# Smaller products in a tiled TensorE: a long convolution's first and last step, and the block maxima of sliding-window attention, placed on other tiles of the array

## The chip, the cores and the metric

The kernel runs as one program on one core of one Trainium2 chip. The time is device microseconds (us) of one execution. The kernel before was timed in three runs: 959.37, 967.51 and 975.18 us, median 967.51.

## The reference

Two independent results are computed and put side by side in the output, 2048 rows of 2 x 576 columns, all in float32:

```python
# left half: attention, H = 32 heads of Dh = 18, S = 2048, window W = 256
q, k, v = split_heads(x @ wqkv)
scores = einsum("bhqd,bhkd->bhqk", q, k) * Dh ** -0.5      # kept where 0 <= q - k < 256
a = merge_heads(einsum("bhqk,bhkd->bhqd", softmax(scores), v)) @ wo
# right half: a state-space convolution, L = 2048, D = 576 channels, N = 128 states
dt = exp(log_dt)
K[d, l] = sum_n real(C[d, n] * exp(dt * (A_re + 1j * A_im) * l)[d, n] * dt * B[d, n])
y = irfft(rfft(pad(u)) * rfft(pad(K)))[:L] + u * Dskip       # transforms of length 4096
concatenate([a, y], -1)
```

## The kernel before

**Taps and projection.** The taps K of the convolution (2048 of them for each of 576 channels) are made from factors: `tables` has phases and exponentials made by matmuls (L414), VectorE, ScalarE and GpSimd, and `taps` (L522) multiplies the factors on TensorE in tiles of 32 columns. Beside it `proj` makes q, k and v with `mm14` (L180), and stores them to a DRAM table `qd` in half-precision pieces. The attention's operands are later loaded from `qd` in units: a unit is four heads and one half of the queries (1024), 16 units in all, each with a Q tile [128, 2, 1024] and a K tile [128, 2, 1280] (`load_unit`, L715 and L716). A head's 54 rows lie on partitions 0 to 53 or 64 to 117, so that two heads share a tile's column.

**The transform.** The convolution is a Fourier transform of u and of K in two steps (32 x 64), a product, and the two inverse steps.
- `s1` (L555 to L567) is the first step. A block is 4 of the 64 values of l, for 144 channels: a tile `src` of 128 partitions (four groups of channels s, with 32 values each) by 576 columns. `w1` is [128, 2, 128]: for each of the two parts, cosine and sine, a block-diagonal matrix with the same 32x32 block for every group. A block takes four matmuls (two parts, two column chunks of 288), each into a PSUM bank of its own, four evacuations of 288 columns, three in four on ScalarE and one in four on VectorE (`evac`, L142), and one store for each part into DRAM: `gx` for u, `gk` for K. `s1_u` (L569) loads each block of u and runs 16 of them, `s1_k` (L578) runs 16 over the taps. The banks come from the pool `pps`, three banks, as long as the projection's pool lives, later from `ring`.
- `conv` (L584 to L681): 16 steps load 2 of the 32 values of f from `gx` and `gk` (`load`, L592 and L596, one step ahead), do the second step (`s2`, L606), multiply on VectorE and GpSimd (L637 to L644), do the first inverse step (`inverse`, L614), and store to a DRAM table `h`. Then 16 last steps (`qd` is the loop variable here): `loadh` (L658) loads four pieces of `h` three steps ahead; four matmuls (L675) with `i2`, a block-diagonal [128, 64], fill two banks of the ring, one for each half of 576 channels; ScalarE evacuates one and VectorE the other, and four stores write 32 rows of 576 columns each into the output.

**Attention.** For each unit, `gmax` (L722 to L754) makes a bound for the softmax: for each of 32 blocks of 32 queries, the scores against the 288 keys that the block can see, and their row maximum over the masked part. A block has four matmuls (L734), one for each head j, on row half j % 2 of the array (64 rows) and column tile j (32 columns), all into one ring bank. Blocks go in pairs, then VectorE reduces each bank in one custom instruction (L741) into a column of `m`. At a unit's end `m` is scaled and transposed to `mt`, and four stores put each head's 1024 values into row 54 or 118 of the unit's Q tile: the scores matmul (L775) then subtracts the bound by itself. `scores` (L775, exponential on ScalarE at L777, mask on GpSimd at L786), `values` (L798) and the normalization follow in items: 16 units x 2 halves x 3 banks are 96 items. The output's product with wo is spread over the last items (`wo_first`, `wo_part`), and its rest, `wo_rest` (L1008, L1042), runs for the third and the fourth chunk of 512 rows at the very end; its operands `oh` and `ol` are loaded at L996.

**What sets the order.** Up to the attention a scheduler orders the instructions that are handed to it by `merge`, which interleaves generators by shares: `merge((proj, 50), (tables, 308), (s1u, 16))`, a share for each step that the generator yields. From `attention_start` on the order is written out by hand: an item takes two steps of scores, about 2.7 steps (pairs) of `gmax`, one of values, some of `conv`, and for the first nine items one block of `s1_k`. Three blocks' worth of `s1_k` (2 + 2 + 1) stand ahead of the items, beside the maxima of unit 0, and two more ahead of that. The ring has three PSUM banks and serves the maxima, the late `s1_k`, all of `conv` and the wo products.

**DMAs.** Nearly all DMAs are issued by SyncE (SP), one behind the other in program order; an issue that waits holds up all behind it. `after(1, ...)` puts a store off until the next item's beginning (`begin`), so that it doesn't stand in the queue before its data is made. The recorded line of a store is then L134. In the queue, stores of the last step show as `out_dram<-t`, the loads of h as `tx<-h` and `ho<-h`, the maxima's as `Q<-mt`, the first step's as `gx<-g` and `gk<-g`, those of the wo product as `out_dram<-ya`, and `den<-osb` is the normalization's.

## Time and profile before

| | before |
|---|---|
| runs, us | 959.37, 967.51, 975.18; median 967.51 |
| the profiled execution, its own time | 969.41 us |
| its span (first to last instruction) | 967.7 us |
| granted TensorE clock, mean | 0.968 |
| busy: PE (TensorE matmuls) | 845.6 us, 87% |
| busy: DVE (VectorE) | 636.2 us, 66% |
| busy: ACT (ScalarE), POOL (GpSimd) | 565.1 and 565.8 us, 58% each |
| bytes moved, mean rate | 145.45 MB, 150 GB/s |

The profile is one execution as the hardware recorded it. PEld is TensorE's weight load, which overlaps with the matmuls. A view by windows gives the busy time of each engine in stretches of the span with its count of instructions, in the order PE, PEld, DVE, ACT, POOL, then the granted clock, the share of the 16 DMA engines and GB/s. The chain of waits starts at the last instruction of a stretch and goes back at each step to what released it, or to the instruction before it on its engine; by line, it says what share of the stretch each line holds on that chain. "PE r L734" is a matmul of line 734 whose output is named r; "SPq" is SP issuing a DMA; "DMA" is a transfer under way; "issue" is time in which an engine waited for nothing recorded. A timeline row has the start, the duration, the engine, the line, output and inputs, tile shapes and the number of instructions or passes, and behind <- what was waited for. Stages of the span, by where the lines appear: to about 90 us loads and set-up; 90 to 398 tables, projection and `s1_u`; 398 to 430 `s1_k` and the maxima of unit 0; 430 to 485 the first nine items with the rest of `s1_k`; 485 to 850 the middle of the convolution beside the attention; 850 to 968 the last steps and the end.

### The profile page before, as it was taken

To read this page: it belongs to the slowest core of one execution; us is meant where nothing else is said; L and a number is where in the kernel's file an instruction comes from. 1 tells how busy PE (TensorE), PEld (TensorE's weight loads), DVE (VectorE), ACT (ScalarE), POOL (GpSimd) and SP (SyncE) were. 2 spreads that over 40 slices of the span, in tenths; PEclk is the share of its full clock that TensorE was granted. 3 is DMA by queue.
4 is the path that set the end of the run, shared out by engine and by line. 5 is a ranking of instruction groups with operands and counts; after the bars stand their busy time and mean duration, and the time that the engine had idled before them with its cause. 6 is when DMAs were issued, how large, how long until landed. Compare 5 with 4: busy or idle time off the path is not lost.

```text
span 967.7 us, 28844 instructions
## 1 busy us (share of the span) xinstructions
PE 845.6 (87%) x11364; PEld 434.8 (45%) x11364; DVE 636.2 (66%) x1745; ACT 565.1 (58%) x917; POOL 565.8 (58%) x679
## 2 busy tenths in 40 slices
PE   4876789888999899889988988889988999999887
PEld 1344445464566556644423333333333444444345
DVE  5988558467664684556577777887777575666434
ACT  2663766556667676335646556566665555565670
POOL 2178758385685695602357776586876666553360
PEclk9987899899999999999999999999999899999899
DMA  9845345334443443553485676865668475477763
GB/s 326 256 98 147 90 118 134 94 81 125 104 123 92 101 117 84 167 177 131 151 174 146 174 175 164 183 174 135 159 149 197 109 185 152 124 186 200 189 188 132
DMA packets 137184, 145.45 MB, mean 150 GB/s; under 512 B 36552, under 2 KB 105336, under 8 KB 136920
## 3 DMA queue, kind: packets, MB, share of 16 engines
q1 hardware_dynamic: 131000, 131.45, 52.3%
q0 software_dynamic: 4592, 10.32, 4.0%
q8 instruction: 89, 1.46, 0.7%
q10 hardware_dynamic: 1456, 1.84, 0.6%
q14 instruction: 47, 0.39, 0.1%
HBM read 81.29 MB, written 61.01 MB: 147 GB/s over the span
## 4 chain that ended last, share of the span: by engine, by line
PE 50%; DVE 13%; issue 10%; DMA 8%; POOL 7%; ACT 7%; SPq 3%; DVEq 0%; ACTq 0%; POOLq 0%
PE pp L180 8%; PE po L798 6%; PE r L734 6%; PE r L606 6%; PE r L1008 5%; PE kp L522 4%; PE ST L775 4%; PE pp L565 3%; PE r L614 3%; DVE jk L741 2%; PE r L565 2%; PE x L414 2%; DMA raw<-in_x_dram 2%; DMA K<-in_wqkv_dram 2%; PE r L675 1%
## 5 line engine op out<-in xcount | busy, mean ns | idle before, releaser
L741 DVE CUSTOM_DVE_ANT_0 jk<-r,bias 128x288 f32<-128x288 f32 (+7 forms) x512 | 198.8, 432 | 98.0 <-PE r L734 97.3
L786 POOL TENSOR_SCALAR_AFFINE_SELECT P<-P 128x512 f32<-128x512 f32 x240 | 156.7, 681 | 164.2 <-ACT P L777 160.8
L777 ACT ACTIVATE P<-ST,esc 128x1024 f32<-128x1024 f32 (+1 forms) x192 | 201.8, 1059 | 73.1 <-PE ST L775 72.5
L484 POOL TENSOR_TENSOR m<-A,tr 128x1024 f32<-128x1024 f32 x72 | 142.2, 1999 | 73.7 <-PE kp L522 73.6
L734 PE MATMUL r<-K,Q 54*32 54x288 f16 (+8 forms) x2048 | 127.0, 285 | 18.6 <-DVE t L637 4.4
L798 PE MATMUL po<-P,V 128*32 128x256 f32 (+2 forms) x1408 | 100.4, 396 | 12.6 <-ACT osb L806 6.0
L734 PEld LDWEIGHTS <-Q 54*32 54x32 f16 x2048 | 46.3, 90 | 112.5 <-issue 87.6
L643 POOL TENSOR_TENSOR Y<-t,t 64x288 f32<-64x288 f32 x64 | 55.7, 871 | 66.1 <-DVE t L638 64.1
L522 PE MATMUL kp<-Q,m 128*32 128x64 f32 x4608 | 80.4, 222 | 12.8 <-DVE Q L505 3.5
L522 PEld LDWEIGHTS kp<-Q,m 128*32 128x32 f32 x4608 | 69.4, 110 | 37.3 <-issue 23.6
L775 PE MATMUL ST<-Q,K 64*128 64x384 f16 (+2 forms) x704 | 73.8, 281 | 3.4 <-ACT oh L858 1.7
L798 PEld LDWEIGHTS po<-P,V 128*32 128x32 f32 x1408 | 35.7, 110 | 47.1 <-issue 23.8
L565 PE MATMUL pp<-ut,w 128*128 128x288 f32 x128 | 41.1, 452 | 17.1 <-ACT g L145 12.4
L644 POOL TENSOR_TENSOR Y<-t,t 64x288 f32<-64x288 f32 x64 | 52.6, 822 | 3.8
L425 DVE TENSOR_TENSOR k<-x,k 128x512 f32<-128x512 f32 (+1 forms) x54 | 33.9, 642 | 30.0 <-ACT k L424 29.5
L426 DVE TENSOR_SCALAR ab<-k 128x512 int32<-128x512 int32 (+1 forms) x54 | 50.8, 951 | 1.7 <-POOL wr L343 1.3
L606 PE MATMUL r<-tk,w 128*64 128x288 f32 x256 | 42.2, 436 | 7.1 <-DVE m L741 7.1
L462 POOL TENSOR_TENSOR tr<-tr,mab 128x768 f32<-128x768 f32 x18 | 34.6, 1920 | 23.6 <-ACT tr L431 23.5
L614 PE MATMUL r<-Y,i 128*128 128x288 f32 x128 | 42.9, 446 | 5.4 <-DVE m L741 2.3
L606 PE MATMUL r<-tx,w 128*64 128x288 f32 x256 | 40.8, 429 | 7.3 <-DVE m L741 3.8
L431 ACT ACTIVATE mg<-x 128x512 f32<-128x512 f32 x72 | 39.7, 599 | 6.8 <-PE x L414 6.4
L364 DVE SCALAR_TENSOR_TENSOR qst<-pp,qst 128x512 f16<-128x512 f32 x30 | 20.6, 686 | 33.3 <-ACT qst L363 29.6
(190 smaller groups left out, 1664.7 us busy)
## 6 DMA issues: line engine op xcount, KB each, us to landing
qd<-qst SPq DMA_DIRECT2D x72, 128.0 KB
gx<-g SPq DMA_DIRECT2D x32, 288.0 KB
gk<-g SPq DMA_DIRECT2D x32, 288.0 KB
tx<-gx SPq DMA_DIRECT2D x32, 288.0 KB
tk<-gk SPq DMA_DIRECT2D x32, 288.0 KB
h<-ho SPq DMA_DIRECT2D x16, 576.0 KB
Q<-qd SPq DMA_DIRECT2D x32, 216.0 KB
raw<-in_x_dram SPq DMA_DIRECT2D x16, 320.0 KB
```

The lines of the kernel that those rows point to most:

```text
L180: self.nc.tensor.matmul(ps, u, v, start=(i == 0), stop=(i == len(ops) - 1))
L484: self.nc.gpsimd.tensor_tensor(m, A[:, ch, a0:a0 + 8].unsqueeze(3).to_broadcast(sh), tr[:, ch, part, 0:8].unsqueeze(2).to_broadcast(sh), o ...
L522: nc.tensor.matmul(kp[32 * st:32 * st + 32, c % 2 * JJ2 + j, :], m[:, ch, a0:a0 + 32], Q[:, ch, term % 2, :], start=(term == 0), stop=(ter ...
L565: nc.tensor.matmul(ps, self.w1[:, part, :], src[:, o:o + k], start=True, stop=True)
L606: nc.tensor.matmul(ps[64 * par:64 * par + 64], w2[:, par, 64 * part:64 * part + 64], t[:, par, 2 * hs:2 * hs + 2, :], start=True, stop=True)
L614: nc.tensor.matmul(pair[par], i1[:, par, :], Y[par], start=True, stop=True)
L734: nc.tensor.matmul(ps[32 * j:32 * j + 32, :n], d["Q"][r, b, 32 * t:32 * t + 32], d["K"][r, b, k0:k0 + n], start=True, stop=True, skip_grou ...
L741: nc.vector.tensor_tensor_reduce(out=jk[:, :n], in0=ps[:, :n], in1=self.bias[:, 288 - n:], scale=1.0, scalar=-3e38, op0=OP.add, op1=OP.max ...
L775: nc.tensor.matmul(ps[:, u, o:o + n], d["K"][h, jp, k0:k0 + 128], d["Q"][h, jp, q0:q0 + n], start=True, stop=True, skip_group_check=True)
L777: nc.scalar.activation(pt[:, 2 * jp:2 * jp + 2, lo:hi], ps[:, :, lo:hi], AF.Exp, scale=self.esc)
L786: nc.gpsimd.affine_select(v, v, pattern=[[0, 4], [sg, 128]], compare_op=OP.is_ge, fill=0.0, base=-1 if far else 0, channel_multiplier=-sg)
L798: nc.tensor.matmul(self.po[32 * j:32 * j + 32, t0 * 128:t1 * 128], V[:, kb * 76 + 19 * j:kb * 76 + 19 * j + 32], pt[:, j, o:o + (t1 - t0) ...
```

## The change

**First step.** `w1` shrinks to the 32x32 block for each part, repeated for the four row groups ([128, 2, 32]). A block of `s1` is done in two halves of two channel groups each. A half takes two banks, and each bank gets four matmuls of 32 rows by 32 columns with 288 columns moving: group s0 + s on row tile s0 + s, and on the four column tiles the two column chunks lg by the two parts. Eight matmuls stand side by side. Then come two evacuations of 288 columns, and two stores, one for each chunk, of 64 partitions x 2 x 288. A half is a step of its own, so the shares of `s1_u` and `s1_k` double.

**Last step.** `i2` shrinks to [128, 32], the 64x32 block for each row half. The four matmuls of 128x64 become eight of 64x32: row half p, column tile 2k + (p ^ hf), so that in the second bank (hf = 1) the two values of p come out the other way round. The output rows of the two column halves thus lie on different partitions, and the stores are eight of 32 rows x 288 columns instead of four of 32 x 576.

**Maxima.** Of a pair of blocks, the odd one writes head j to column tile j ^ 1, so that the pair's eight matmuls lie on eight different tiles (2 row halves x 4 column tiles). In `m` the columns of odd blocks are then swapped between heads 0 and 1, and 2 and 3, and in `mt`, behind the transpose, every other row: a head's values are stored by two DMAs of 16 rows each (every other row of 32) instead of one.

```diff
@@ -42,10 +42,7 @@
     tau = 2 * np.pi
     l1, l2, f1, f2 = np.arange(32), np.arange(64), np.arange(32), np.arange(64)
     ph = -tau * np.outer(l1, f1 + 0.25) / 32
-    w1 = np.zeros((128, 2, 128))
-    for s in range(4):
-        w1[s * 32:s * 32 + 32, 0, s::4] = np.cos(ph)
-        w1[s * 32:s * 32 + 32, 1, s::4] = np.sin(ph)
+    w1 = np.tile(np.stack([np.cos(ph), np.sin(ph)], 1), (4, 1, 1))
     w2 = np.zeros((128, 32, 128))
     i1 = np.zeros((128, 32, 128))
     for f in range(32):
@@ -56,10 +53,7 @@
         i1[0:64, f, 0:64], i1[64:128, f, 0:64] = co.T, si.T
         i1[0:64, f, 64:128], i1[64:128, f, 64:128] = -si.T, co.T
     ph = tau * np.outer(f1 + 0.25, l1) / 32
-    i2 = np.zeros((128, 64))
-    for p in range(2):
-        i2[p * 64:p * 64 + 32, p * 32:p * 32 + 32] = np.cos(ph) / 2048
-        i2[p * 64 + 32:p * 64 + 64, p * 32:p * 32 + 32] = -np.sin(ph) / 2048
+    i2 = np.tile(np.concatenate([np.cos(ph), -np.sin(ph)]) / 2048, (2, 1))
     mult = {"c_cm": np.arange(64), "c_ct": np.arange(32) + 0.5, "c_ca": np.r_[64 * np.arange(8), 512 * np.arange(4)],
             "c_cp": np.r_[np.zeros(8), np.full(4, 31.5)]}
     for nm, v in mult.items():
@@ -555,16 +549,26 @@
         yield from self.taps(n - 1)
 
 
-    def s1(self, src, g, l0, nl, pool):
-        nc, n = self.nc, nl * 144
-        for part in range(2):
-            st = self.p[pool].tile([128, n], F32, name="g1")
-            k = n // 2 if n <= 576 else n // 3
-            for o in range(0, n, k):
-                ps = self.p[self.s1_banks[0]].tile([128, 512], F32, name=self.s1_banks[1])[:, :k]
-                nc.tensor.matmul(ps, self.w1[:, part, :], src[:, o:o + k], start=True, stop=True)
-                self.evac(st[:, o:o + k], ps)
-            nc.sync.dma_start(g[part, :, l0:l0 + nl], st.rearrange("p (l j) -> p l j", j=144))
+    def s1(self, src, g, l0, pool):
+
+
+        nc = self.nc
+        for s0 in (0, 2):
+            st = self.p[pool].tile([128, 2, 288], F32, name="g1")
+            bank = [self.p[self.s1_banks[0]].tile([128, 512], F32, name=self.s1_banks[1])[:, :288] for _ in range(2)]
+            for s in range(2):
+                r = slice(32 * (s0 + s), 32 * (s0 + s) + 32)
+                for o in range(4):
+                    lg, part = divmod(o, 2)
+                    nc.tensor.matmul(bank[s][32 * o:32 * o + 32], self.w1[r, part, :], src[r, lg * 288:lg * 288 + 288],
+                                     start=True, stop=True, skip_group_check=True)
+            for s in range(2):
+                self.evac(st[:, s], bank[s])
+            for lg in range(2):
+                l = l0 + 2 * lg
+                nc.sync.dma_start(g[:, :, l:l + 2].rearrange("a (f s) l j -> (a f) s (l j)", s=4)[:, s0:s0 + 2],
+                                  st[64 * lg:64 * lg + 64])
+            yield
 
     def s1_u(self):
         uv = self.a["u"].rearrange("(p l) (s j) -> s p l j", l=64, j=144)
@@ -572,14 +576,12 @@
             ut = self.p["s1u"].tile([128, 4, 144], F32, name="ut")
             for st in range(4):
                 self.nc.sync.dma_start(ut[32 * st:32 * st + 32], uv[st][:, l0:l0 + 4, :])
-            self.s1(ut.rearrange("p l j -> p (l j)"), self.gx, l0, 4, "s1s")
-            yield
+            yield from self.s1(ut.rearrange("p l j -> p (l j)"), self.gx, l0, "s1s")
 
     def s1_k(self):
         kf = self.K.rearrange("p l j -> p (l j)")
         for b in range(16):
-            self.s1(kf[:, b * 576:(b + 1) * 576], self.gk, 4 * b, 4, "s1k")
-            yield
+            yield from self.s1(kf[:, b * 576:(b + 1) * 576], self.gk, 4 * b, "s1k")
 
     def conv(self):
         nc, a, tt = self.nc, self.a, self.nc.vector.tensor_tensor
@@ -672,13 +674,17 @@
             pair = [ring() for hf in range(2)]
             for hf in range(2):
                 for k in range(2):
-                    nc.tensor.matmul(pair[hf][64 * k:64 * k + 64], self.i2, hp[:, k, hf * 288:hf * 288 + 288],
-                                     start=True, stop=True)
+                    for p in range(2):
+                        r, o = slice(64 * p, 64 * p + 64), 64 * k + 32 * (p ^ hf)
+                        nc.tensor.matmul(pair[hf][o:o + 32], self.i2[r], hp[r, k, hf * 288:hf * 288 + 288],
+                                         start=True, stop=True, skip_group_check=True)
             nc.scalar.activation(y[:, 0:288], pair[0], AF.Copy)
             nc.vector.tensor_copy(y[:, 288:576], pair[1])
             yield
             for k in range(4):
-                self.after(1, nc.sync.dma_start, outv[4 * qd + k], y[32 * k:32 * k + 32])
+                for hf in range(2):
+                    cs = slice(288 * hf, 288 * hf + 288)
+                    self.after(1, nc.sync.dma_start, outv[4 * qd + k][:, cs], y[32 * (k ^ hf):32 * (k ^ hf) + 32, cs])
 
 
     def att_setup(self):
@@ -731,7 +738,8 @@
             n = 32 * t + 288 - k0
             for j in range(4):
                 r, b = slice(64 * (j % 2), 64 * (j % 2) + 54), j // 2
-                nc.tensor.matmul(ps[32 * j:32 * j + 32, :n], d["Q"][r, b, 32 * t:32 * t + 32], d["K"][r, b, k0:k0 + n],
+                o = 32 * (j ^ t % 2)
+                nc.tensor.matmul(ps[o:o + 32, :n], d["Q"][r, b, 32 * t:32 * t + 32], d["K"][r, b, k0:k0 + n],
                                  start=True, stop=True, skip_group_check=True)
             pair.append((t, n, ps))
             if t % 2 == 0:
@@ -749,8 +757,10 @@
         nc.vector.transpose(mt, m16)
         for j in range(4):
             r = 64 * (j % 2) + 54
-            self.after(1, nc.sync.dma_start, d["Q"][r:r + 1, j // 2].rearrange("o (s q) -> o s q", q=32),
-                       mt[32 * j:32 * j + 32])
+            for e in range(2):
+                o = 32 * (j ^ e) + e
+                self.after(1, nc.sync.dma_start, d["Q"][r:r + 1, j // 2].rearrange("o (s e q) -> o e s q", e=2, q=32)[:, e],
+                           mt[o:o + 31:2])
         yield
 
     BL = [(0, 0, 0, 1), (128, 2, 0, 3), (512, 1, 0, 2), (768, 4, 2, 4), (1024, 3, 1, 4), (1408, 5, 3, 4)]
@@ -910,7 +920,7 @@
-                streams.append((part(s1k, 1), 1))
+                streams.append((part(s1k, 2), 2))
@@ -1052,7 +1062,7 @@
-            self.w1 = cp.tile([128, 2, 128], F32, name="w1")
+            self.w1 = cp.tile([128, 2, 32], F32, name="w1")
@@ -1076,10 +1086,10 @@
-                merge((proj, 50), (tables, 308), (s1u, 16))
+                merge((proj, 50), (tables, 308), (s1u, 32))
-            for _ in part(s1k, 2):
+            for _ in part(s1k, 4):
@@ -1087,11 +1097,11 @@
-                merge((part(gm, 8), 8), (part(s1k, 2), 2))
+                merge((part(gm, 8), 8), (part(s1k, 4), 4))
-                merge((gm, 10), (part(s1k, 2), 2))
+                merge((gm, 10), (part(s1k, 4), 4))
-                for _ in part(s1k, 1):
+                for _ in part(s1k, 2):
@@ -1103,7 +1113,7 @@
-                    self.i2 = self.p["fc"].tile([128, 64], F32, name="i2")
+                    self.i2 = self.p["fc"].tile([128, 32], F32, name="i2")
```

Two places show how instructions move. On **TensorE ahead of the first item**, a block of `s1_k` (to the pool `pps`, three banks) stands between the maxima of unit 0 (L734, then L742) and the first scores (ST). Before:

```order
L734 LDWEIGHTS Q_5866
L734 MATMUL r<-K_5867,Q_5866 32x288
L565 MATMUL pp<-K,w_62 128x288 x4
L775 LDWEIGHTS K_5867
L775 MATMUL ST<-Q_5866,K_5867 128x384
```

and in the changed kernel:

```order
L742 LDWEIGHTS Q_6118
L742 MATMUL r<-K_6119,Q_6118 32x288
L563 MATMUL pp<-K,w_62 32x288 x24
L785 LDWEIGHTS K_6119
L785 MATMUL ST<-Q_6118,K_6119 128x384
```

The one block of four matmuls has become three halves of eight: its own two, and the last half of the block ahead of it, which lay inside the maxima and now stands behind them.

On **SP's queue in the last step** (`t` is the output tile y; mt are the maxima of the last unit; ya is the wo product's output), before:

```order
L134 DMA out_dram<-t_13231 32x576 x4
L658 DMA tx<-h 32x2x576 x4
L134 DMA Q_5874<-mt 1x32x32 x4
L134 DMA out_dram<-t_13330 32x576 x4
L134 DMA out_dram<-ya 128x576
```

and in the changed kernel:

```order
L128 DMA out_dram<-t_13735 32x288 x8
L660 DMA tx<-h 32x2x576 x4
L128 DMA Q_6126<-mt 1x16x32 x8
L128 DMA out_dram<-t_13838 32x288 x8
L128 DMA out_dram<-ya 128x576
```

The order of the groups is the same; the stores of y and of mt have twice as many instructions, and the loads of h stand behind them as before.

## The prediction

> **What bounds the kernel now.** First the page: how full the engines are. Then the busy time by stage, and the chain of waits of each stage, which says where a saved microsecond of TensorE would be felt.
>
> ```profile
> PE 845.6 (87%) x11364; PEld 434.8 (45%) x11364; DVE 636.2 (66%) x1745; ACT 565.1 (58%) x917; POOL 565.8 (58%) x679
> ...
> 90.00:398.00 308.00, 279.99 (x5609) 174.99 (x5607) 192.56 (x294) 197.51 (x357) 207.07 (x163) 0.97 0.42 103
> 398.00:430.00 32.00, 24.79 (x196) 14.77 (x196) 15.10 (x76) 9.80 (x23) 4.92 (x9) 0.95 0.59 197
> 430.00:485.00 55.00, 51.00 (x574) 25.22 (x575) 32.76 (x167) 35.57 (x54) 15.82 (x27) 1.00 0.46 151
> 485.00:850.00 365.00, 327.24 (x3692) 136.61 (x3692) 265.51 (x963) 215.02 (x321) 246.56 (x357) 0.98 0.67 161
> 850.00:968.00 118.00, 104.05 (x1081) 53.89 (x1078) 57.62 (x165) 61.53 (x90) 44.78 (x71) 0.97 0.65 177
> ```
>
> The first figure after the length is TensorE. It is busy 88 to 93% of every stage from 90 us on but for 398 to 430; the next engine is VectorE at 73% in 485 to 850. The five stages are: tables, projection and the first step over u; the first step over K beside the first maxima; the rest of K inside attention; the convolution's middle; its last step and the end. Their chains, in that order:
>
> ```profile
> by line: PE pp L180 24.2%; PE kp L522 12.2%; PE pp L565 7.1%; issue 6.7%; PE x L414 5.7%; DMA raw<-in_x_dram 3.2%; DMA ut<-in_u_dram 2.6%; DVE Q L505 2.5%; DVE Q L507 2.4%; DVE qst L364 2.3%; SPq L186 2.0%; ACT K L530 2.0%; DVE ab L426 2.0%
> ...
> by line: PE pp L565 32.0%; DMA K<-qd 21.1%; issue 12.1%; PE r L734 11.0%; DVE jk L741 7.6%; DMA Q<-mt 5.4%; DVE m L741 3.6%; DVE K L692 3.6%; SPq L134 1.9%; PE r L565 1.4%; SPq L715 1.1%; SPq L716 1.0%; PE ST L775 1.0%; DVE mt L749 0.7%; DV
> ...
> by line: PE r L565 35.7%; PE r L734 13.4%; PE po L798 11.3%; DMA tx<-gx 10.5%; issue 9.0%; DVE jk L741 6.5%; PE ST L775 6.0%; SPq L134 4.0%; DVE m L741 3.1%; ACT P L777 2.3%; SPq L592 1.6%; SPq L596 1.2%; DVE m L748 1.1%; ACT osb L806 1.1%;
> ...
> by line: PE r L606 15.2%; PE po L798 11.0%; PE r L734 11.0%; issue 10.5%; PE r L614 7.7%; PE ST L775 6.7%; PE r L1008 4.9%; DVE jk L741 3.5%; POOL P L786 3.3%; POOL Y L644 2.8%; DMA tx<-gx 2.8%; ACT P L777 2.5%; POOL Y L643 2.4%; DVE osb L8
> ...
> by line: PE r L1008 28.4%; PE po L798 13.0%; PE r L675 11.8%; issue 6.2%; PE ST L775 6.2%; PE r L734 5.3%; DMA den<-osb 3.4%; SPq L658 2.5%; DVE osb L857 2.4%; DMA out_dram<-t 2.0%; SPq L134 1.7%; DMA Q<-mt 1.5%; SPq L842 1.5%; DVE ya L1042
> ```
>
> All three lines that the change packs tighter (L565, L734, L675) stand on the chain. So I take a stage's gain as the line's chain time, times the share of its matmul time that goes. What the chain hardly shows is SP's queue, which only issues DMAs. Its timeline from 866 us on is what I read last, and it decides most of what follows.
>
> **The change part by part: TensorE.** What a group of matmuls takes, by its number of concurrent tiles:
>
> ```profile
> 416.71 2.21 PE L565 MATMUL pp<-K,w 128*128 128x288 f32 x8
> 610.05 0.71 PE L606 MATMUL r<-tx,w 128*64 128x288 f32 x4
> 602.15 1.07 PE L798 MATMUL po<-P,V 128*32 128x384 f32 x16
> 845.76 0.30 PE L734 MATMUL r<-K,Q 54*32 54x288 f16 x4
> 851.39 0.43 PE L734 MATMUL r<-K,Q 54*32 54x288 f16 x8
> 864.86 1.19 PE L675 MATMUL r<-ho,i 128*64 128x288 f32 x8
> ```
>
> An f32 matmul is recorded as two passes. L565's four matmuls are eight passes one behind the other: 2.21 us. L606 has two matmuls side by side on two column tiles: four passes in 0.71 us, so two rounds. L798 runs four column tiles at once: 16 passes of 384 (and fewer) columns in 1.07 us. So column tiles do run at once. L734 shows it with row halves mixed in: one block's four matmuls take 0.30 us, and a second block on the same four tiles adds 0.13.
>
> (1) First step (s1). A block's four matmuls of 2.21 us become two groups of eight on eight tiles, each two rounds: 0.71 by L606, 1.42 together. That is 0.79 us or 36% less for each of 32 blocks. Evacuations stay four per block at the same widths, so ACT and DVE gain nothing.
> In 90 to 398, L565 holds 7.1% of 308 us, 21.9; times 0.36, **8 us**.
> In 398 to 430 the chain has 10.2 us of L565, of which the first two blocks lie under a load of K:
>
> ```profile
> 405.76 0.23 PE L734 MATMUL r<-K,Q 54*32 54x32 f16 x7 [1.93 <-DMA K<-qd]
> ...
> 427.04 2.49 SPq L134 DMA_DIRECT2D Q<-mt  x4
> ...
> 428.80 0.32 PE L775 MATMUL ST<-Q,K 64*128 64x384 f16 x1 [0.89 <-DMA Q<-mt]
> ```
>
> The maxima start at 405.76 when K lands, whatever s1 takes ahead of it. The five blocks behind it give 5 x 0.79 = 4.0 us of TensorE. Short groups also let VectorE work through the three buffers it has, instead of idling through 2.2 us, so I take **6**. Against this, the first unit's Q<-mt becomes eight issues instead of four, and the scores at 428.80 wait for them: 2.49 us more, so **3.6 net**.
> In 430 to 485, L565 holds 35.7% of 55, 19.6; times 0.36, **7 us**.
>
> (2) Maxima. A pair of blocks falls from 0.43 towards 0.30 us (30%), when both banks are free. Where the second block waits for VectorE to empty a bank, nothing is gained. In 485 to 850 L734 has 11.0% of 365 us on the chain, 40.2; 30% is 12, and I take about half, **6.5**, since VectorE (73% busy) and its three banks come next. Bounds: 0 if every second block waits, and 256 pairs x 0.13 = 33 if none does and all of it shows.
>
> (3) Last step (i2). Four matmuls in two rounds of pairs (1.19 us) become one group of eight, 0.71: about 40% of 13.9 us on the chain (11.8% of 118), or 5.6 us, if TensorE still sets the pace there. By (4) it does not, so I count **0**.
>
> **The change part by part: SP.** Every DMA is issued by SP one after the other. The change issues four stores per s1 block instead of two, eight mt stores per unit instead of four, and eight output stores per last step instead of four: 64 + 64 + 64 more. Bytes stay the same.
>
> ```profile
> L134 SPq DMA_DIRECT2D Q<-mt x64: 502/589/1742, 427.0 to 911.1; - x64
> L134 SPq DMA_DIRECT2D out_dram<-t x64: 315/420/1723, 866.0 to 950.2; - x64
> ...
> 866.03 2.43 SPq L134 DMA_DIRECT2D out_dram<-t  x4
> 868.56 3.54 SPq L658 DMA_DIRECT2D tx<-h  x4
> 872.20 2.44 SPq L134 DMA_DIRECT2D Q<-mt  x4
> ...
> 899.02 2.45 SPq L842 DMA_DIRECT2D den<-osb  x4
> 901.51 0.58 SPq L134 DMA_DIRECT2D out_dram<-ya  x1
> ...
> 911.75 0.57 SPq L996 DMA_DIRECT2D oh<-od  x1
> 912.37 0.42 SPq L996 DMA_DIRECT2D ol<-od  x1
> 912.89 1.77 SPq L658 DMA_DIRECT2D ho<-h  x4
> ...
> 926.70 1.79 SPq L658 DMA_DIRECT2D tx<-h  x4
> 928.59 5.57 SPq L134 DMA_DIRECT2D out_dram<-t  x12
> ...
> 943.86 0.43 SPq L996 DMA_DIRECT2D ol<-od  x1
> ```
>
> An output store of 32 rows costs SP 0.42 us and 0.46 with the step to the next (5.57/12); a load of h 0.45, an mt store 0.61. The half-wide store still has 32 rows, so I take 0.46; the change's trace alone can show it.
>
> (4) From 866.0 to 928.5 SP issues 11 sets of output stores, 11 of loads, two of mt, one of den, three ya, two pairs of oh and ol. At those prices this is 44 x 0.464 + 44 x 0.45 + 8 x 0.61 + 2.45 + 1.4 + 1.8 = 50.8 us of 62.5: SP is 81% full already, waiting 11.7. The change doubles the stores and the mt: 88 x 0.464 + 44 x 0.45 + 16 x 0.61 + 5.65 = **76.0 us**. No slack is left. The loads of h for step 15 stand last in that row of work; three steps of prefetch let TensorE run ahead only until SP falls behind. So, against the old clock and without the gains, the last load is issued at 866.0 + 76.0 = 942.0, and lands 1.7 us later (the 1.74 us that the chain gives Q<-mt at 909.85, below), at 943.8. Step 15 now starts at 933.81:
>
> ```profile
> 909.85 1.74 DMA Q<-mt
> ...
> 933.81 1.19 PE L675 MATMUL r<-tx,i 128*64 128x288 f32 x8
> ```
>
> That is **10.0 us late**, and the 33.9 us behind step 15 (two more items, the last norm, wo_rest) follow it. A second way to the same end: SP still has three sets of stores (11.1) ahead of oh and ol of the third chunk, and one more (3.7) ahead of the fourth's, which then issue at 958.4 instead of 943.86; two runs of 72 matmuls at 0.125 us (9 us each) behind 955.7 give 973.7, with the old 3.6 us of stores 977.3. Both say 977.7 for 967.7.
>
> In other stages I cost the added issues at nothing: s1's 64 come over the 395 us up to 485, one in 6 us, and the maxima's 64 over the 480 us from 427 to 911, one in 7.5; the loads behind them in the queue are issued an item or more ahead, which hides them. If that cover failed, about half a microsecond would be felt for each that stands ahead of a load in need, at most a few us.
>
> The sum: 967.7 - 8 - 3.6 - 7 - 6.5 + 10 = **952.6 us** of span. The profiled execution itself took 969.41 for a span of 967.7, and the median of the runs is 967.51; minus 15.1 that gives 952.4, which I round to **953 us**.
>
> The page "TensorEngine Tiling (Array Packing)" of the Trainium skill (Gotcha 1: PSUM Pressure) speaks against two of the parts: different row tiles, it says, cannot use the same PSUM bank simultaneously, and both the maxima and the last step put two row halves into one bank. The trace speaks for the change: L734's block of four already has both halves in one bank, in different quadrants, and takes 0.30 us in all. By the page (2) would give 0 and the sum would be 959.
>
> **The rivals.**
> *TensorE sets the end, not SP.* Half-wide stores could cost SP less, or the issues could fall into its 11.7 us of waits. Then the 10 us go and (3) counts: 967.7 - 25.1 - 5.6 = 937 of span, 937 as a median. For it: 11.7 us of slack is there. Against it: the added work in that stretch is 25.2 us, more than twice the slack, and no row shows an issue below 0.3 us. The Trainium skill's page "DMA: Bandwidth & Descriptors" (Issuing engines are not separate DMA queues) would side with this rival: it calls the time a sequencer takes to start a DMA usually small relative to the DMA itself. Here the rows have it at 0.42 to 0.59 us apiece and the queue nearly full, so the page's "usually" does not carry this stretch.
>
> *Eight tiles don't run at once.* No row shows more than four. If a group of eight took two groups' time, s1, maxima and last step would give nothing, and the SP terms would stay: 967.7 + 2.5 + 10 = 980, slower by 1.3%. For it: no row with f32 on row tiles. Against: column tiles and row halves each run at once already.
>
> *SP goes at its present mean pace*, the rival on the slow side. If SP's waits belong to the DMAs (each waits for an earlier one to land) and not to TensorE, every issue costs what one costs now: 62.5 us over 107 of them, 0.584. The same stretch then has 159 issues: 92.9 us, and the oh and ol issues behind it move out likewise (34 more at 0.584, 978.8), so that wo_rest ends near 997 instead of 977; less 25.1 this is 972, slower than now. It decides from a pace of about 0.56 us on. For it: tx<-h at 868.56 took 3.54 instead of 1.79. Against: that one waited for the buffer that the last step frees.
>
> **How the numbers follow.** I give SP at issue price 0.55, TensorE at the end 0.19, no packing 0.10, SP at the mean pace 0.16. A measurement of this kernel tells 2% from no change at best (its runs lie from 959.37 to 975.18), so faster means below 948. That takes nearly all of the second case (0.18) and a quarter of the first (0.14), where s1 may give up to 13 + 7 + 10 and the maxima up to double: 0.32. Slower by over 2% needs 987: parts of the last two, 0.06. The rest, 0.62, is within. The range goes down to the middle of the TensorE case, 936, and up to 976, past the slow SP case.
>
> **What would show it.** Right: s1 groups of 16 passes at about 0.7 us; pairs of the maxima at 0.30 to 0.33; eight output stores of 3.7 us; SP with hardly a gap from about 841 (866 less the 25.1 us gained) on; and L675's successor waiting for loads of h. Wrong: output stores below 0.35 us apiece, groups of 16 at 1.4 us, a tail from step 0 to the end no longer than the present 114 us, or a first stage that does not shrink.

## The result and the profile after

The changed kernel took 1022.54 us (median of four runs, 1020.61 to 1027.3), the kernel before on the same chip 968.82 (959.37 to 975.18): a ratio of 1.0596, 95% interval 1.0505 to 1.0687. That is 6% slower; 953 was forecast, with a range of 936 to 976. In the changed kernel the first step's matmul is L563, the maxima's L742, the second step's L608, the scores' L785, the last step's L679; SP's deferred stores are L128, the loads of h L660. The profiled execution of it took 1020.91 us, its span is 1019.2.

The page of the changed kernel, its engines and the row of granted clock in 40 slices of 25.5 us:

```profile
PE 854.8 (84%) x12260; PEld 403.3 (40%) x12260; DVE 642.6 (63%) x1745; ACT 562.6 (55%) x917; POOL 562.7 (55%) x679
...
PEclk9988998999999998557799899999989999999779
```

TensorE's busy time went up, 845.6 to 854.8 us, though at the full clock each changed group of matmuls is shorter. The clock row says why that can be: slices 17 to 20 (408 to 510 us) have 5, 5, 7, 7.

To see where the 51.5 us of span went I cut both executions at the same places of the program: the last taps matmul (398, 401 us), the first instruction of the second step on TensorE's queue, a wait (489.3, 506.4), that of the last step (852.5, 878.2) and the end. The windows' last three columns are granted clock, DMA share and GB/s. Before:

```profile
90.00:398.00 308.00, 279.99 (x5609) 174.99 (x5607) 192.56 (x294) 197.51 (x357) 207.07 (x163) 0.97 0.42 103
398.00:489.30 91.30, 78.61 (x811) 41.12 (x810) 51.11 (x256) 47.91 (x79) 23.05 (x41) 0.98 0.53 170
489.30:852.50 363.20, 326.92 (x3682) 136.70 (x3682) 263.01 (x950) 214.31 (x320) 245.34 (x355) 0.98 0.67 160
852.50:968.00 115.50, 101.55 (x1051) 52.66 (x1047) 56.86 (x163) 59.71 (x88) 43.70 (x68) 0.97 0.64 176
```

And the changed kernel:

```profile
90.00:401.00 311.00, 272.69 (x5737) 157.50 (x5736) 192.58 (x292) 196.39 (x358) 210.95 (x170) 0.97 0.47 105
401.00:506.40 105.40, 88.89 (x1194) 25.32 (x1194) 52.92 (x255) 46.43 (x79) 18.49 (x32) 0.61 0.59 141
506.40:878.20 371.80, 329.61 (x3685) 138.29 (x3685) 266.87 (x952) 214.33 (x320) 243.35 (x354) 0.96 0.64 156
878.20:1019.20 141.00, 102.59 (x1179) 51.17 (x1175) 56.25 (x163) 59.85 (x88) 42.51 (x68) 0.92 0.53 148
```

So: tables +3, first step over K and first maxima +14 at a clock of 0.61, middle +9, tail +26. In the tail TensorE has the same 102 us of work in 141 us instead of 115: it waits. The waits of TensorE behind 860 us, first before, then changed (us in total, times, longest):

```profile
PE po L798 <- issue: 2.7, 3, 1.6
...
PE ST L775 <- DMA Q<-mt: 0.4, 1, 0.4
```

```profile
PE ST L785 <- DMA Q<-mt: 11.7, 2, 10.8
PE r L679 <- DMA ho<-h: 7.2, 6, 2.0
```

And the timeline of SP in the changed kernel's tail, with the two TensorE rows around the long wait:

```profile
892.82 3.91 SPq L128 DMA_DIRECT2D out_dram<-t  x8
896.83 1.78 SPq L660 DMA_DIRECT2D tx<-h  x4
...
947.53 3.61 SPq L128 DMA_DIRECT2D out_dram<-t  x8
951.24 4.96 SPq L128 DMA_DIRECT2D Q<-mt  x8
...
975.70 1.78 SPq L660 DMA_DIRECT2D tx<-h  x4
977.57 12.66 SPq L128 DMA_DIRECT2D out_dram<-t  x24
```

```profile
942.50 0.39 PE L785 MATMUL ST<-Q,K 64*128 64x384 f16 x4
953.72 0.26 PE L785 MATMUL ST<-Q,K 64*128 64x128 f16 x1 [10.82 <-DMA Q<-mt]
```

The last unit's maxima were done at 924 and transposed to mt by 932, but their stores stand in SP's queue behind sets of eight output stores and are issued from 951.24 on; the scores that need them stop TensorE for 10.8 us. (The mt stores in the two orders of SP's queue under "The change" are those of the unit before it, issued here at 898.71.) From the first output store to the long last set SP takes 84.75 us (892.82 to 977.57); before it was 62.56 (866.03 to 928.59).

The tighter groups are there, at the prices that were forecast. Changed kernel, TensorE:

```profile
208.80 0.69 PE L563 MATMUL pp<-ut,w 32*32 32x288 f32 x8
215.59 0.71 PE L563 MATMUL pp<-ut,w 32*32 32x288 f32 x16
417.25 1.21 PE L563 MATMUL pp<-K,w 32*32 32x288 f32 x16
703.17 0.30 PE L742 MATMUL r<-K,Q 54*32 54x288 f16 x4
704.30 0.32 PE L742 MATMUL r<-K,Q 54*32 54x288 f16 x8
941.01 0.72 PE L679 MATMUL r<-ho,i 64*32 64x288 f32 x16
```

Sixteen passes of the first step take 0.71 us, of the last step 0.72, a pair of blocks of the maxima 0.32. The third row is the catch: at 417 us the same sixteen take 1.21.

### The profile page after: what moved, and what is told of

Same layout as the page of the kernel before. It is cut to its first block, busy times and chain, and to the rows that moved or that the text cites. A ratio compares the mean times of both kernels' runs of the same rounds, so it can differ in the third digit from the quotient of the medians.

```text
span 1019.2 us, 30976 instructions
## 1 busy us (share of the span) xinstructions
PE 854.8 (84%) x12260; PEld 403.3 (40%) x12260; DVE 642.6 (63%) x1745; ACT 562.6 (55%) x917; POOL 562.7 (55%) x679
## 4 chain that ended last, share of the span: by engine, by line
PE 33%; DVE 7%; issue 5%; SPq 5%; DMA 5%; ACT 3%; POOL 1%; DVEq 0%; ACTq 0%; POOLq 0%
PE po L808 6%; PE r L742 6%; PE r L608 6%; PE r L1018 5%; PE ST L785 4%; PE r L616 3%; SPq L128 3%; DMA ho<-h 2%; PE r L563 2%; DVE jk L749 2%; ACT P L787 1%; DVE osb L867 1%; DVE t L641 1%; PE r L679 1%; DVE spread L859 1%
## 5 line engine op out<-in xcount | busy, mean ns | idle before, releaser
L749 DVE CUSTOM_DVE_ANT_0 jk<-r,bias 128x288 f32<-128x288 f32 (+7 forms) x512 | 201.3, 432 | 125.5 <-PE r L742 124.2
L796 POOL TENSOR_SCALAR_AFFINE_SELECT P<-P 128x512 f32<-128x512 f32 x240 | 154.4, 671 | 209.7 <-ACT P L787 207.3
L742 PE MATMUL r<-K,Q 54*32 54x288 f16 (+8 forms) x2048 | 126.0, 308 | 21.9 <-DVE m L749 5.5
L808 PE MATMUL po<-P,V 128*32 128x256 f32 (+2 forms) x1408 | 108.0, 422 | 13.6 <-issue 6.2
L742 PEld LDWEIGHTS <-Q 54*32 54x32 f16 x2048 | 45.0, 91 | 134.0 <-issue 112.7
L785 PE MATMUL ST<-Q,K 64*128 64x384 f16 (+2 forms) x704 | 78.7, 295 | 14.8 <-DMA Q<-mt 14.8
L608 PE MATMUL r<-tx,w 128*64 128x288 f32 x256 | 42.5, 441 | 14.2 <-DVE m L749 8.5
L608 PE MATMUL r<-tk,w 128*64 128x288 f32 x256 | 43.2, 445 | 9.7 <-DVE m L749 9.7
L420 DVE TENSOR_SCALAR ab<-k 128x512 int32<-128x512 int32 (+1 forms) x54 | 47.5, 889 | 1.7 <-POOL wr L337 1.3
L785 PEld LDWEIGHTS <-K 64*128 64x128 f16 x704 | 22.3, 96 | 58.7 <-issue 25.1
L174 PE MATMUL pp<-xh,wh 128*128 128x512 f16 x150 | 41.8, 402 | 4.0 <-DVE qst L358 3.1
```

Of the source, the lines that this page charges most:

```text
L608: nc.tensor.matmul(ps[64 * par:64 * par + 64], w2[:, par, 64 * part:64 * part + 64], t[:, par, 2 * hs:2 * hs + 2, :], start=True, stop=True)
L742: nc.tensor.matmul(ps[o:o + 32, :n], d["Q"][r, b, 32 * t:32 * t + 32], d["K"][r, b, k0:k0 + n], start=True, stop=True, skip_group_check=True)
L749: nc.vector.tensor_tensor_reduce(out=jk[:, :n], in0=ps[:, :n], in1=self.bias[:, 288 - n:], scale=1.0, scalar=-3e38, op0=OP.add, op1=OP.max ...
L785: nc.tensor.matmul(ps[:, u, o:o + n], d["K"][h, jp, k0:k0 + 128], d["Q"][h, jp, q0:q0 + n], start=True, stop=True, skip_group_check=True)
L796: nc.gpsimd.affine_select(v, v, pattern=[[0, 4], [sg, 128]], compare_op=OP.is_ge, fill=0.0, base=-1 if far else 0, channel_multiplier=-sg)
L808: nc.tensor.matmul(self.po[32 * j:32 * j + 32, t0 * 128:t1 * 128], V[:, kb * 76 + 19 * j:kb * 76 + 19 * j + 32], pt[:, j, o:o + (t1 - t0) ...
```

## Experiments

Two theories stood against two others. **A**: the granted clock follows how much of the array works, not how long TensorE is busy, so the small products pull it to half. Its rival **B**: the half-clock stretch comes of the maxima, of SP, of idle gaps, or by chance. **SP**: the tail is longer because of the added issues. Its rival: the products themselves (two row halves in one bank, eight tiles), or smaller DMA pieces, cost the time. All ratios are to the kernel before on the same chip, with the 95% interval; four or ten runs each.

### The parts one by one

`s1_only` takes the hunks of `w1`, `s1`, `s1_u`, `s1_k` and their shares alone, `gmax_only` those of `gmax`, `i2_only` those of `i2` and of the output stores. Their cores:

```diff
# s1_only
-                nc.tensor.matmul(ps, self.w1[:, part, :], src[:, o:o + k], start=True, stop=True)
+                    nc.tensor.matmul(bank[s][32 * o:32 * o + 32], self.w1[r, part, :], src[r, lg * 288:lg * 288 + 288],
+                                     start=True, stop=True, skip_group_check=True)
# gmax_only
+                o = 32 * (j ^ t % 2)
# i2_only
+                        r, o = slice(64 * p, 64 * p + 64), 64 * k + 32 * (p ^ hf)
```

> The kernel before with the change's first step alone (s1 of u and of K in 32x32 products); maxima and last step as before. Theory A (the granted clock follows how much of the array works, not how long it is busy): the half-clock stretch of about 61 us between 400 and 500 us is there, since s1's blocks of 128x128 are what is missing in it; that costs 12 to 15 us, the tables' stage gains nothing, and the tail is as before: 975 to 985 us. Rival B (the stretch comes of the whole change, for example of the maxima's denser pairs or of SP's longer queue, or is there by chance): no half-clock stretch over 10 us here, and 955 to 968 us.

> The kernel before with the maxima's odd blocks on the other four tiles alone, with eight mt stores instead of four. Theory A: no half-clock stretch over 10 us at 400 to 500 us. In the middle the pairs whose banks are free start 0.014 us apart instead of 0.132, but VectorE sets the pace, so what the pairs gain is waited for at the second step; in the tail SP has 8 issues of 0.6 us more (4.9 of its 11.7 us of waits), which is covered: 962 to 970 us. Rival B: a half-clock stretch appears here, 975 to 985. Rival C (the forecast's 6.5 us for the maxima is right): about 961.

> The kernel before with the last step alone in 64x32 products and eight half-wide output stores. SP theory (SP's queue sets the tail): SP needs 88 x 0.46 + 44 x 0.45 + 8 x 0.61 + 5.65 = 71.2 us for the issues that took 62.5, and with some waits left about 75: the tail is 9 to 16 us longer, 977 to 984 us in all. Rival (the tail's 26 us come of the maxima's stores, or of low clock only): 963 to 970 us.

Measured: `s1_only` 983.76 us (1.0166, 1.0123 to 1.0209), `gmax_only` 984.16 (1.0171, 1.0132 to 1.0209), `i2_only` 995.15 (1.0282, 1.0235 to 1.0329). Each part alone is slower, with an interval clear of 1 (only that of `i2_only` lies wholly above 2%); the three losses add up to 62 us against 54 for the whole. The windows of `s1_only`, then of `gmax_only`:

```profile
395.00:430.00 35.00, 26.80 (x487) 9.83 (x487) 15.89 (x75) 8.67 (x22) 4.68 (x9) 0.58 0.79 189
430.00:465.00 35.00, 32.63 (x388) 9.26 (x388) 17.08 (x88) 16.52 (x27) 5.71 (x10) 0.54 0.47 115
```

```profile
395.00:430.00 35.00, 26.97 (x185) 15.44 (x185) 15.46 (x75) 9.57 (x22) 5.31 (x9) 0.85 0.53 180
430.00:465.00 35.00, 32.45 (x337) 16.67 (x337) 19.37 (x103) 20.84 (x33) 6.71 (x11) 0.95 0.41 142
```

The stretch comes with the first step alone: the clock's record has 61.4 us of half clock there in one piece, as in the changed kernel, and not in `gmax_only`, which has single windows of it. From the last taps to the second step `s1_only` takes 103.1 us instead of 91.5. That speaks for A against the maxima, SP and chance; idle gaps are left to the fills below. What was missed: `gmax_only` was to lose nothing and lost 17 us. That is the time that B gave it, but without B's stretch; in its profiled execution, 11 us longer than the one before, the tail accounts for 6.2 (121.3 us for 115.1) and the stretch from the last taps to the second step for 7.3 (98.8 for 91.5), with 15 us of single half-clock windows there for 3.4. Its middle is 364.0 for 363.2, so the pairs gave nothing where 6.5 us were forecast. `i2_only` was to lose 9 to 16 and lost 28: the tail takes 136.6 us.

### The stores given to ScalarE

```diff
# act_stores, on top of the changed kernel
-                    self.after(1, nc.sync.dma_start, outv[4 * qd + k][:, cs], ...
+                    self.after(1, nc.scalar.dma_start, outv[4 * qd + k][:, cs], ...
```

> The changed kernel with the last step's eight output stores issued by ScalarE instead of SP; all else of the change stays. SP theory: SP is left with 44 loads and 16 mt issues, about 35 us of work in the stretch; the 10.8 us wait of the scores for Q<-mt and the waits for loads of h go, and the tail falls from 141 us to 115 or less: 990 to 998 us. Rival (the smaller pieces of the stores load the DMA engines, whoever issues them, or the low clock makes the tail): 1012 to 1025 us.

Measured: 1032.42 us (1.0678, 1.0633 to 1.0723), slower still. This expectation failed. The waits of ScalarE behind 860 us:

```profile
ACT P L787 <- DMA out_dram<-t: 37.7, 12, 4.4
ACT t L681 <- PE r L679: 9.3, 2, 8.4
```

The eight issues of a set take ScalarE 3.7 us or so, and the exponentials of the scores stand behind them: 37.7 us of waiting in front of P. The issue cost moved to an engine whose work the tail waits for. Nor was SP set free: from 880 to 990 us, 55 us of its waits are put down to the landing of output stores, 30 of them ahead of loads of h, and TensorE still waits 8.8 us for mt. What ties SP's issues to those stores was not looked into. So this run neither bears out the SP theory nor refutes it.

### Only the issues, and only the products

`split_stores` is the kernel before with its outputs written by eight half-wide stores, all products as they were. `i2_swapped_h` has the products of the change and four stores: the second column half of h is written with neighbouring rows swapped, so that the outputs lie in order.

```diff
# split_stores, on top of the kernel before
-                self.after(1, nc.sync.dma_start, outv[4 * qd + k], y[32 * k:32 * k + 32])
+                for hf in range(2):
+                    cs = slice(288 * hf, 288 * hf + 288)
+                    self.after(1, nc.sync.dma_start, outv[4 * qd + k][:, cs], y[32 * k:32 * k + 32, cs])
# i2_swapped_h, on top of i2_only
-                self.after(1, nc.sync.dma_start, self.h.rearrange("a l f d -> (a l) f d")[:, 2 * fp:2 * fp + 2, :], ho)
+                self.after(1, nc.sync.dma_start, ...[:, 2 * fp:2 * fp + 2, 0:288], ho[:, :, 0:288])
+                for e in range(2):
+                    self.after(1, nc.sync.dma_start, self.h.rearrange("a (l e) f d -> e (a l) f d", e=2)[1 - e]
+                               [:, 2 * fp:2 * fp + 2, 288:576], ho[e:e + 127:2, :, 288:576])
```

> The kernel before with nothing changed but the last step's output stores: eight of half the width instead of four. SP theory: the same 64 issues more in the tail as in i2_only, hence the same loss: the tail 15 to 25 us longer, 985 to 997 us. Rival (it is the last step's products, two row halves in one bank or the eight tiles, that cost the time): 965 to 972 us.

> The last step alone in 64x32 products on eight tiles, but h is written with the second column half of neighbouring rows swapped (three DMAs instead of one for each of 16, in the middle), so that the outputs come out in order and four full stores do. SP theory: the tail has its old 44 stores, the loss of 28 us goes, and the last step's products give up to the forecast 5.6 us: 960 to 970 us. Rival (two row halves in one bank, or the eight tiles, cost something): 975 us or more.

Measured: `split_stores` 991.34 us (1.0241, 1.0177 to 1.0305), `i2_swapped_h` 972.05 (0.9991, 0.9957 to 1.0025; the kernel before had 971.72 in its runs). The waits of TensorE in the tail, `split_stores` first:

```profile
PE ST L777 <- DMA Q<-mt: 6.8, 2, 6.5
PE r L675 <- DMA out_dram<-t: 4.0, 2, 2.2
```

```profile
PE ST L777 <- DMA Q<-mt: 4.2, 2, 3.8
PE po L800 <- issue: 2.7, 3, 1.6
```

The split of the stores alone, without any change to a matmul, costs 22.6 us; the products alone cost nothing, and gain nothing that the runs tell from zero (the median is 2 us above the range of the SP theory and 3 below the rival's; the tail of the profiled execution is 111.5 us, 3.6 less than before). From the first output store to the last long set SP takes 82.6 us in `split_stores` and 63.0 in `i2_swapped_h`. The last unit's mt, once it is made, stands 9 us before its first issue in the kernel before, 10 in `i2_swapped_h` and 20 in `split_stores`. This settles the rival: neither the eight tiles nor two row halves in one bank are to blame. The smaller pieces of the half-wide stores went with the added issues in both, so their own share isn't told apart here; the 6.2 us that the tail of `gmax_only` loses with eight issues more, whose pieces are no smaller, says that issues count by themselves.

### The maxima without their stores in the tail

```diff
# gmax_last_plain, on top of gmax_only: the last two units as before the change
-                o = 32 * (j ^ t % 2)
+                o = 32 * (j ^ (t % 2 if i < 14 else 0))
```

with four stores for those two units. `i2_gmax` is this and `i2_swapped_h` together.

> The maxima alone as in gmax_only, but the last two units, whose mt stores fall among the last step's, keep the old placing and four stores each. SP theory: the 5.6 us wait of the scores for Q<-mt in the tail goes, the tail is back at 115 us from 121, and the time is 5 to 7 us under gmax_only's 984: 975 to 980 us. Rival (the tail's loss has another cause): as gmax_only, 981 to 987 us. If it is at 966 to 970, the maxima's loss was in the tail alone.

> The last step with swapped h and four stores, and the maxima on eight tiles but for the last two units: the two parts of the change without the issues that they add to the tail. SP theory: at or below the kernel before, 958 to 970 us. Rival: the sum of what the two parts lose apart from SP's queue, 975 us or more.

Measured: `gmax_last_plain` 974.81 us (1.0055, 1.0019 to 1.0091), `i2_gmax` 980.2 (1.0105, 1.0041 to 1.0168). The waits of TensorE in the tail of `gmax_only`, then of `gmax_last_plain`:

```profile
PE ST L779 <- DMA Q<-mt: 6.5, 2, 5.6
```

```profile
PE ST L783 <- DMA Q<-mt: 1.5, 2, 1.1
```

Eight issues fewer in the tail, and the tail is back at 115.4 us; for the tail the SP theory holds. Each against the kernel before on its own chip, the loss falls from 17.2 us to 3.1, by more than the 5 to 7 us of the tail. The stretch from the last taps to the second step, in which the two kernels don't differ, took 93.7 us here for 98.8 in `gmax_only`, so part of that kernel's 17 us isn't the change's. What is left, half a per cent by the ratio, says that the denser pairs don't pay in the middle either. `i2_gmax` missed its expectation and came out in the rival's range: its tail is fine (114.0 us), but its middle took 372.0 us. So did that of `i2_only` (372.0), which changes nothing there, while `act_stores`, with the whole change, had 364.7 and the other kernels 363 to 369. The length of the middle goes with its clock: of the four kernels with 369 to 372 us it has 26 to 31 us at half clock, of the other ten 7 to 20. What sends these windows to half isn't shown, and I can't tie the middle's 9 us in the changed kernel to the change.

### What holds the clock

`s1_u_only` keeps K's blocks as before and takes the new first step for u alone, with the nonzero blocks of the old `w1`. `s1_fill` is `s1_only` with four added full-array matmuls (`extra`) in each half of a K block, `s1_fill_small` with as many on one 32x32 tile, `s1_fill_more` with more of the full ones in the first eight halves. The added results are overwritten by the products.

```diff
# s1_fill, on top of s1_only, in each half of s1_k
+            for _ in range(extra):
+                nc.tensor.matmul(bank[0], self.fill[:, 0:128], self.fill, start=True, stop=True, ...)
# s1_fill_small
+                nc.tensor.matmul(bank[0][0:32], self.fill[32 * s0:32 * s0 + 32, 0:32], self.fill[32 * s0:32 * s0 + 32], ...)
# s1_fill_more
+            yield from self.s1(kf[:, b * 576:(b + 1) * 576], self.gk, 4 * b, "s1k", 12 if b < 4 else 4)
```

> The kernel before with the new first step for u alone (with the nonzero 32x32 blocks of the old w1), K's as before. Theory A: no half-clock stretch between 400 and 500 us, since K's blocks keep the whole array; the tables' stage gives none of the forecast 8 us, since what TensorE saves there is waited for elsewhere: 963 to 971 us. Rival (the first step over u costs something of its own, through its stores or the scheduler's order): 972 to 980 us.

> The first step alone in 32x32 products, with four added f16 matmuls of 128x128 by 288 columns of a constant in each half of a K block (128 in all; their results are overwritten at once by the products). They cost 128 x 0.125 = 16 us of TensorE at the full clock, 32 at half. Theory A (the clock follows how much of the array works): the 61 us stretch of half clock goes, or breaks up into single windows, and the time stays at 975 to 985 us or falls in spite of the added work. Rival (the gate goes by TensorE's idle gaps or by chance): the stretch stays and the added work comes on top, about 1000 us.

> The same with the 128 added matmuls on one 32x32 tile, 288 columns each: as many instructions and as much time on TensorE, a sixteenth of the array. Theory A: the half-clock stretch stays, about 60 us or longer, and the added work at half clock comes on top: 995 to 1015 us. Rival (the clock follows TensorE's busy time, whatever the size): as with the large ones, the stretch goes.

Measured: `s1_u_only` 973.49 us (1.0058, 1.0018 to 1.0099), `s1_fill` 997.21 (1.0313, 1.0238 to 1.0389), `s1_fill_small` 1011.66 (1.0452, 1.0387 to 1.0516). With K's blocks on the whole array the stretch is gone (clock 0.85, 0.90 and 0.95 in the three windows of 35 us from 395 on), but the time of `s1_u_only` is in the rival's range: the new first step over u gives nothing and costs about half a per cent. `s1_fill_small` is as A expected. With four full-array fills the stretch stayed, 64.9 us: the expectation of A failed in that form. To see why, I worked out an index from the traces of all 14 kernels. The clock's switches lie on a grid of 3.413 us. For each such window: the columns that the matmul passes streamed, counted twice for f32, times the rows x columns in use / (128 x 128), summed and divided by 8192. That is close to what the full array streams here: f16 passes of 288 columns follow each other in 0.1225 us, which makes 8024 columns in 3.413 us. Then what the clock was in the next window:

```
index        windows at half clock:        windows at full clock:
             full in the next one          half in the next one
0    - 0.20     0 of  98                     83 of   83
0.20 - 0.25     0 of  26                     33 of   36
0.25 - 0.30     1 of  31                     32 of   50
0.30 - 0.35    28 of  62                     28 of   69
0.35 - 0.40    39 of  56                     16 of  133
0.40 - 0.45    37 of  41                      1 of  192
over 0.45      87 of  87                      0 of 2851
```

One bound near a third tells both directions apart, with a mixed band from 0.25 to 0.45 around it. Busy time doesn't do it: of 287 windows at half clock in which TensorE was busy over 90%, 103 stayed at half. At the same busy time it is the index that decides: of 197 windows at half clock with TensorE busy over 98%, all 22 with an index below 0.30 stayed there, and 105 of the 106 at 0.40 or above came back. That leaves idle gaps out too. The Trainium skill's page "TensorE: Matmul & The Clock Gate" (Part 1) has the gate set by how busy TensorE has been in windows of 3.4 us, with half and full as its two states; windows and states agree with this trace, busy time as the measure does not. In `s1_only` and in the changed kernel the windows from 401 to 443 us lie at 0.24 or below, in the kernel before at 0.31 to 0.62. In `s1_fill` nearly all up to 468 were at 0.19 to 0.30: the dose was too small. So the next run gave three times the dose for a while.

> As s1_fill, but with 12 added matmuls instead of 4 in each half of the first four K blocks (8 halves), 4 in the rest. An index of the array's work (over each 3.41 us of the clock's record: columns times two for f32, times rows and columns of the tile, as a share of what the full array streams) stood at 0.23 to 0.30 in s1_fill's stretch, and over all runs the clock came back in nearly every window above 0.40 and never below 0.30. Theory A in this form: 12 fills take the windows to 0.37 or more, so the clock is back within three or four windows and holds with 4 fills (0.45 to 0.55 at full clock in s1_fill from 475 us on): half clock for 20 us or less instead of 65, and 970 to 990 us in spite of 64 more fills. Rival (the stretch ends by itself after some 60 us): the stretch stays, and the added work makes it 1005 to 1020 us.

Measured: 991.17 us (1.0226, 1.0173 to 1.0279). Windows of `s1_fill`, `s1_fill_small` and `s1_fill_more`:

```profile
430.00:465.00 35.00, 33.61 (x352) 11.17 (x344) 15.93 (x79) 10.05 (x20) 1.88 (x3) 0.50 0.54 137
```

```profile
465.00:500.00 35.00, 33.72 (x368) 12.54 (x364) 11.98 (x60) 14.37 (x22) 7.87 (x15) 0.55 0.42 99
```

```profile
400.00:405.00 5.00, 2.66 (x18) 1.69 (x19) 0.31 (x1) 1.03 (x1) 2.60 (x7) 0.76 0.80 177
405.00:440.00 35.00, 30.41 (x464) 15.35 (x463) 14.83 (x73) 7.85 (x21) 0.00 (x0) 0.99 0.64 155
440.00:460.00 20.00, 18.95 (x196) 5.95 (x195) 9.73 (x50) 7.82 (x12) 1.88 (x3) 0.50 0.54 136
460.00:510.00 50.00, 45.19 (x714) 17.69 (x714) 26.72 (x127) 28.49 (x43) 14.05 (x25) 0.99 0.49 116
```

With twelve fills the clock was back after one window and stayed for 35 us, index 0.30 to 0.77; where they end (four from there on) two of three windows were at 0.30 and 0.27, and it was gone for 20 us, until the items' other matmuls raised the index to 0.33 and 0.47. By the medians the sixty-four matmuls more made it 6 us faster than `s1_fill`, though the intervals of the two ratios overlap. The time is 1 us above the range expected, and that the clock would hold with four fills was wrong; that the dose decides is shown, both ways, and in `s1_fill_small` as many small fills as `s1_fill` has left 116 us of half clock. A holds in the form of the index. `s1_fill_more` is faster neither than the kernel before nor than `s1_only`: the fills cost about what the clock gives.

## Why the prediction was wrong

The span came out 66.6 us above the forecast one (1019.2 for 952.6): 24.7 of it in the first step over K with the first maxima (+14 for -10.6), 15.8 in the tail, 15 in the middle and 11 in the tables.

**Prices of the products: right.** The first step at 0.71 for 16 passes, the last at 0.72 and the maxima's pair at 0.32 are what was taken from L606 and L734. The worry over two row halves in one bank, from the page "TensorEngine Tiling (Array Packing)" of the Trainium skill (Gotcha 1), didn't come true: the last step has that in each of its banks, in different rows of the bank, and takes 0.72 us.

**First step, 398 to 485, -3.6 and -7: wrong in sign; this is the step that failed first.** "The line's chain time, times the share of its matmul time that goes" takes for granted that what is left runs as fast as before; the clock was a term put at nothing. The blocks of 128x128 were most of the array's work in that stage (by the index 90% in 398 to 430 us, 63% up to 489); without them the clock fell at the first pause (index 0.03 at 398 us) and did not come back for 61.4 us. The stage took 14 us more instead of 10.6 less. The prediction read the granted clock in its window rows (0.95 in 398 to 430) and made nothing of it.

**First step over u, -8: not there.** TensorE's busy time in this stage fell from 280.0 to 272.7 us (the windows above), but the taps end at 400.1 to 407.6 us in the seven kernels with the new `s1_u` and at 393.1 to 397.8 in the seven without. The waits of TensorE from 90 to 402 us, before and after:

```profile
PE pp L565 <- ACT g L145: 5.1, 3, 3.1
...
PE kp L522 <- issue: 3.3, 5, 1.4
...
PE x L414 <- DVE k L425: 2.4, 3, 1.1
```

```profile
PE kp L516 <- issue: 9.8, 6, 2.6
PE x L408 <- DVE k L419: 8.8, 5, 4.1
PE pp L563 <- DMA ut<-in_u_dram: 3.2, 1, 3.2
```

What was saved came back as waits for nothing recorded in the taps' runs, for VectorE, and for the loads of u. That other chains run just beside TensorE's, so that a chain's share is no gain, is my reading of it. What the waits for nothing are (TensorE now has four times the first step's instructions) was not tried and stays open.

**Maxima, -6.5: 0.** The pairs whose banks are free start 14 ns apart instead of 132, as forecast, but they are few: 48 of the middle's 178 pairs in `gmax_only`, at most 48 x 0.12 = 5.8 us of TensorE, and none of it shows in its middle of 364.0 us. That VectorE's pace is the bound, the lower end of that term, is likely but not shown: in 510 to 860 us the second step's wait for it is 10.2 us before, 11.8 in `gmax_only` and 18.2 in the changed kernel, but also 15.0 in `i2_only`, without denser pairs. Their stores in the tail, costed inside SP's sum, took about 6 us by themselves.

**SP, +10: the mechanism and the price right, the size wrong.** Eight output stores take 3.6 to 3.9 us where SP doesn't wait (3.7 forecast), and the queue sets the tail. But 76.0 us of issues were 84.75 us of queue, of which 4.8 are recorded as waits of SP, and "10 us late" took step 15, behind its loads of h, for the one reader of the queue that counts. (Its second way to the 10 us adds up to 977.3, not 977.7.) The runs show another reader: the last unit's scores, which wait 10.8 us for mt. By itself this is 10.4 us more than before (0.4). The tail grew by 25.8 us; `i2_only` and `gmax_only` give 21.5 and 6.2 of it. The rival's bound, SP at 0.584 us per issue, was 92.9; the measured pace is 84.75 / 159 = 0.533, between the two.

**Rivals.** TensorE setting the end, and no packing, both fell: the tail grew, and sixteen passes take 0.71 us. That no packing was nearest by its number, 980, is chance. SP at its mean pace, 972, was nearest in its mechanism, and it too had counted the 25 us of gains. None had the clock.

## What to carry to other kernels

Packing small products tighter takes work off the array, and in these traces the clock goes by that work: before making a stage's matmuls smaller, work out from the trace what share of the full array the stage still streams in 3.4 us, and keep it well above a third. Count the DMA issues that a new layout of tiles brings, and look at who stands behind them in the queue, above all near the end; here the last step's cost was in 64 stores, and a swap made upstream, where the queue has room, took it away. A queue that was 81% full had no slack to count on, and handing its issues to ScalarE, an engine on the path, was worse.

## What the runs showed of the hardware beyond that

- Half clock lasted on while the work stayed small: 61.4 us in one piece in two kernels, 78.5 in `act_stores`, 81.9 in `s1_fill_small`, with TensorE recorded as busy for 86 to 94% of it.
- The recorded busy time of TensorE hides this: 32.63 of 35 us at a clock of 0.54 in `s1_only`, 32.09 of 35 at 1.00 before.
- Issuing a DMA costs ScalarE as much as SP: eight output stores take 3.70 us on ScalarE (883.34 in `act_stores`) and 3.61 to 3.91 on SP (947.53 and 892.82 in the changed kernel).
